# The last layer's bias added ahead of the transposes, and single stores in the last round

## The chip, the cores and the metric

The kernel runs on one core of one Trainium2 chip. Its time is the device time of one execution in microseconds (us), the median of several runs. TensorE (PE) multiplies into PSUM, ScalarE (ACT) and VectorE (DVE) do elementwise work, GpSimd (POOL) fills a few constants, and the queues of SyncE (SP) and ACT issue DMA transfers.

## The reference

A cross network of six layers on 4096 rows of 416 columns, in bfloat16:

```python
def reference(x0, ws, bs):          # x0 [4096, 416], ws [6, 416, 416], bs [6, 416]
    x = x0
    for l in range(ws.shape[0]):
        x = x0 * (x @ ws[l] + bs[l]) + x
    return x
```

With x = x0 * c, where c is a factor that starts at one, each layer is c <- c + (x @ ws[l] + bs[l]), and then x = x0 * c. So the kernel keeps the factor c beside x, and the output is x0 * (c + x @ ws[5] + bs[5]).

## The kernel before

**Layout.** Layers 0 to 4 work on transposed data: columns of the network on the 128 partitions, rows of the batch along the free dimension. 416 columns are three blocks of 128 (m = 0, 1, 2) and a remainder of 32. `XM0` holds x0 transposed, `CM` the factor c transposed, `XH` three half-batch buffers of x; `XR[0]`, `CR` and `XR` hold the same for the remainder, with the four groups of 512 rows stacked on the partitions. The batch has two halves, s = 0 and 1, of 2048 rows. The last layer (`LL` = 5) works on rows: 128 rows of the batch on the partitions, 416 columns free, so that its results can be stored as they are.

**A layer of the middle.** The six tiles (s, m) are named A = (0,0), B = (0,1), C = (0,2), D = (1,0), E = (1,1), F = (1,2). For each, TensorE fills two PSUM tiles of 128x1024 (`mm_full`, line 209; `mm_row`, line 215, for the remainder's share), taking them in pairs (`layer_products`). PSUM has room for four such tiles. ACT evicts each with its bias into a buffer of `t` (a pool of six), VectorE adds it to `CM` and multiplies by `XM0` into `XH`.

**The last such layer**, layer 4, is written out in `feeding_layer`, with VectorE's order given by hand: `pin` keeps a call in program order. `evict` is line 333, `add` line 341, `mul` line 345. It also prepares the last layer: a tile's factor `c` gets the last layer's bias (`last_bias`, line 349) and is then transposed by DMA from SP's queue into rows, `XLrows` (`xl_dmat`, line 232). The remainder goes through `CR`, `rem_out` and `scrR`, and ACT copies it to `XLrows` in `xl_rem` (line 312): `xl_rem(0)` just ahead of E's evictions, in `before_last`, and `xl_rem(1)` after F's. In the kernel before, `last_bias` covers all 2048 rows of a tile of s = 0, but for s = 1 only the first half of each group of 512, by a strided view of 4x256:

```python
            if s:
                c = c.rearrange("p (g r) -> p g r", g=NG)[:, :, 0:CW // 2]
```

**The last layer.** It has 32 blocks of 128 rows, in eight quads (s, i) of four blocks g; four rounds take two quads each. In each round TensorE forms eight products in eight PSUM banks: `mm_q_full` (line 464) for the three blocks of columns, `mm_q_rem` (line 477) for the remainder. For the two quads of s = 1 and i >= 2, that is, for the last round, `mm_q_rem` also adds the bias, as a product of a row of ones and the row `bLr` (line 481), since those rows of `CM` have no bias. ACT copies a product from PSUM to a buffer of `t` (line 507), VectorE adds `XLrows` (line 511) and multiplies by `X0rows` into an output tile (line 494, `close_product`, one block late), and the tile is stored (line 496). The first three rounds work by pairs of blocks, 128x832. The last round (`ENDS`) closes its eight blocks, u = 0 to 7, one at a time. For u >= 5 TensorE adds the factor itself, by products of `CM` and `CR` with an identity (lines 468 and 470), and line 511 falls away; u = 7 is multiplied by VectorE straight from PSUM. In the last round u = 0 to 5 are stored in pairs and u = 6 alone from SP's queue, u = 7 alone from ACT's.

The order of all of it is the program's order on each engine; waits between engines come from the tiles that they share. On SP the eight transposes of layer 4 stand ahead of all stores, in both kernels.

Of the kernel before, what the change touches and what calls it, by code (L numbers as in the profile page):

```python
# [9 lines left out]
ACT = mybir.ActivationFunctionType  # L10
ALU = mybir.AluOpType
BF16 = mybir.dt.bfloat16
# [4 lines left out]
def kernel(  # L17
# [7 lines left out]
    nc = tc.nc  # L25
    B, D = x0.shape
    L = ws.shape[0]
    P = 128
# [3 lines left out]
    NS = 2  # L32
    NG = 4
    CW = 512
    SW = NG * CW
# [11 lines left out]

    ident = const.tile([P, P], BF16)
    dz = const.tile([P, 2], FP32)
    ones = const.tile([P, P], BF16)  # L50
    WM = const.tile([P, L, NK, D], BF16)
    WR = const.tile([P, L, D], BF16)
    WD = const.tile([P, L, NG, R], BF16)
    bsb = const.tile([L, 4 * P], BF16)
    bLr = const.tile([P, D], BF16)
    bM = const.tile([P, NK, L], FP32)
    bR = const.tile([P, L], FP32)
    X0rows = big.tile([P, NBT, D], BF16)
# [21 lines left out]
    def pin(ins):  # L80
        tc.keep_in_program_order(ins)
# [18 lines left out]
    warm4 = nc.const_aps.tensor(1.0, [P, CW], FP32)  # L100
    nc.vector.memset(dz[:], 0.0)
    make_identity(nc, ident[:])
    nc.gpsimd.memset(ones[:], 1.0)
    nc.gpsimd.memset(WD[:], 0.0)

    load_x0t(0, 0)
# [21 lines left out]
        load_wr(nc.sync, g, 1, L)  # L128
    for l in range(2, L):
        load_wm(nc.sync, l)  # L130
    for q in range(18):
        b0, b1 = NBT * q // 18, NBT * (q + 1) // 18
        nc.sync.dma_start(X0rows[:, b0:b1, :], x0_v[:, b0:b1, :])
    for g in range(NG):
        nc.sync.dma_start(bLr[32 * g:32 * g + 1, :], bs[LL:LL + 1, :])

    def fill_wd(l0, l1):
        for g in range(NG):
# [92 lines left out]
    def xl_dmat(s, k):  # L231
        nc.sync.dma_start_transpose(out=XLrows[:, 16 * s:16 * s + 16, 128 * k:128 * k + 128],
                                    in_=CM[:, k, SW * s:SW * s + SW])
# [73 lines left out]
    def xl_rem(s):  # L307
        dst = XLrows[:, 16 * s:16 * s + 16, NK * P:D].rearrange("p (g i) r -> p i g r", g=NG)
        src = scrR[s][:].rearrange("p i (g r) -> p i g r", g=NG)
        n = 4 if s else 2  # L310
        for i in range(0, 4, n):
            pin(nc.scalar.copy(dst[:, i:i + n], src[:, i:i + n]))
# [13 lines left out]
    def feeding_layer(l, cur, curR, nxt, nxtR):  # L326
        tiles = [(s, m) for s in range(NS) for m in range(NK)]
        pts, ts = {}, {}

        def evict(t):  # L330
            for h in range(2):
                ts[t + (h,)] = tpool.tile([P, 2 * CW], BF16, name="t")
                nc.scalar.activation(ts[t + (h,)][:], pts[t][h][:].rearrange("p a b -> p (a b)"), ACT.Identity,  # L333
                                     bias=bM[:, t[1], l:l + 1], scale=1.0)

        def c_of(t, h):
            c0 = col0(t[0], 2 * h)
            return CM[:, t[1], c0:c0 + 2 * CW]

        def add(t, h):  # L340
            pin(nc.vector.tensor_tensor(out=c_of(t, h), in0=ts[t + (h,)][:], in1=c_of(t, h), op=ALU.add))  # L341

        def mul(t, h=0, n=2):
            c0, w = col0(t[0], 2 * h), n * CW
            pin(nc.vector.tensor_tensor(out=nxt[t[0]][:, t[1], 2 * CW * h:2 * CW * h + w], in0=CM[:, t[1], c0:c0 + w],  # L345
                                        in1=XM0[:, t[1], c0:c0 + w], op=ALU.mult))

        def last_bias(c, bias):
            pin(nc.vector.tensor_scalar(out=c, in0=c, scalar1=bias, scalar2=None, op0=ALU.add))

        def rows_out(t):
            s, m = t
            c = CM[:, m, SW * s:SW * s + SW]
            if s:
                c = c.rearrange("p (g r) -> p g r", g=NG)[:, :, 0:CW // 2]
            last_bias(c, bM[:, m, LL:L])
            xl_dmat(s, m)

        A, Bt, C, Dt, E, F = tiles
        layer_products(l, 0, tiles, pts, cur, curR, evict)  # L360
        evict(Bt)
        pr2 = psum.tile([P, 2, CW], FP32, tag="ps", name="pr2")
        for s in range(NS):
            mm_rem(l, s, pr2[:, s, :], cur, curR)
        tr = []
        for s in range(NS):
            tr.append(tpool.tile([P, 2 * CW], BF16, name="t"))
            for a in range(0, CW, CW // 2):
                nc.scalar.activation(tr[s][:, a:a + CW // 2], pr2[:, s, a:a + CW // 2], ACT.Identity, bias=bR[:, l:l + 1], scale=1.0)

        def rem(s, op):
            part = slice(CW * s, CW * s + CW)
            if op == ALU.add:
                pin(nc.vector.tensor_tensor(out=CR[:, part], in0=tr[s][:, 0:CW], in1=CR[:, part], op=op))
            else:
                pin(nc.vector.tensor_tensor(out=nxtR[:, part], in0=CR[:, part], in1=XR[0][:, part], op=op))

        def rem_out(s):
            last_bias(CR[:, CW * s:CW * s + (CW // 2 if s else CW)], bR[:, LL:L])
            nc.sync.dma_start_transpose(out=scrR[s][:], in_=CR[:, CW * s:CW * s + CW])  # L380

        add(A, 0)
        mul(A, 0)
        add(A, 1)
        add(Bt, 0)
        mul(A, 1)
        add(Bt, 1)
        rows_out(A)
        rem(0, ALU.add)
        mul(Bt, 0, 4)  # L390
        rem(0, ALU.mult)
        rem(1, ALU.add)
        rem_out(0)
        rows_out(Bt)
        rem(1, ALU.mult)

        layer_products(l, 2, tiles, pts, cur, curR, evict)
        evict(Dt)
        add(C, 0)
        add(C, 1)  # L400
        rem_out(1)
        mul(C, 0, 4)
        add(Dt, 0)
        add(Dt, 1)
        rows_out(C)
        mul(Dt, 0, 4)

        def before_last(t):
            xl_rem(0)
            evict(t)  # L410

        layer_products(l, 4, tiles, pts, cur, curR, before_last)
        evict(F)
        add(E, 0)
        rows_out(Dt)
        add(E, 1)
        mul(E, 0, 4)
        add(F, 0)
        add(F, 1)
        rows_out(E)  # L420
        mul(F, 0, 4)
        xl_rem(1)
        return lambda: rows_out(F)
# [22 lines left out]
    l = LL  # L446
# [25 lines left out]

    def mm_q_rem(q, py, done):
        s, i = quads[q]
        biased = s == NS - 1 and i >= 2
        for g in range(NG):
            nc.tensor.matmul(py[g][:, 0:D], lhsT=curR[32 * g:32 * g + 32, CW * s + 128 * i:CW * s + 128 * i + 128],  # L477
                             rhs=WR[32 * g:32 * g + 32, l, :], start=(g >= done), stop=(not biased and g < done),
                             tile_position=(32 * g, 0))
        for g in range(NG if biased else 0):  # L480
            nc.tensor.matmul(py[g][:, 0:D], lhsT=ones[32 * g:32 * g + 1, :],  # L481
                             rhs=bLr[32 * g:32 * g + 1, :], start=False, stop=(g < done), tile_position=(32 * g, 0))

    pending, outs = [], []

    def rows(q, g0, n):
        s, i = quads[q]
        b0 = 16 * s + 4 * g0 + i
        return slice(b0, b0 + 4 * (n - 1) + 1, 4)

    def close_product():
        while pending:
            src, q, g0, n, o, j, last, eng = pending.pop()
            pin(nc.vector.tensor_tensor(out=o[:, j:j + n, :], in0=src, in1=X0rows[:, rows(q, g0, n), :], op=ALU.mult))  # L494
            if last:
                eng.dma_start(out_v[:, rows(q, g0 - j, j + n), :], o[:, 0:j + n, :])

    def ew(q, g0, srcs, o, j, last, eng, added, direct):
# [20 lines left out]
    for q, at, done in rounds:  # L519
        tiles = [psum.tile([P, 2, CW], FP32, tag="ps", name=f"py{n}") for n in range(4)]  # L520
        bank = [tiles[n][:, a, :] for n, a in at]

        final = q + 2 == NQ

        def close(groups):
            u = groups[0][0]
            srcs = [tiles[at[g[0]][0]][:, at[g[0]][1]:at[g[0]][1] + len(g), 0:D] for g in groups]
            paired = final and u < 6
            j = u % 2 if paired else 0
            if not j:  # L530
                outs.append(opool.tile([P, 2, D], BF16, name="o"))
            ew(q + u // 4, u % 4, srcs, outs[-1], j, bool(j) or not paired, nc.scalar if final and u == 7 else nc.sync,
               final and u >= 5, final and u == 7)

        for u in range(done):
            if q == 0:
                mm_q_open(q, u, bank[u])
            else:
                mm_q_full(q, u, bank[u], False)
        mm_q_rem(q, bank[0:4], done)  # L540
        close([range(done)])
        if q == 0:
            last_rows_out()
        mm_q_rem(q + 1, bank[4:8], 0)
        for u in range(done, 8):
            mm_q_full(q + u // 4, u % 4, bank[u], True, final and u >= 5)
            if at is ENDS:
                close([[u]])
            elif u % 2:
                close([[u - 1, u]] if at is PAIRS else [[u - 1], [u]])  # L550
# [31 lines left out]
```

## Time and profile before

| | |
|---|---|
| median of 3 runs | 128.86 us (128.81 to 128.91) |
| the profiled execution | 129.12 us, its span 127.3 us |
| granted TensorE clock | 1.0 |
| busy: PE, DVE, ACT | 122.9, 102.4, 88.3 us |
| last byte of the last store written | 126.14 us |
| last landing | 126.51 us |

The span runs from the first to the last instruction that the profiler saw; the execution's time has some 1.8 us more around it. All times in what follows count from the span's start. Rows of groups give line, engine, operation, out<-in, partitions x elements and type, count, then busy us and mean ns of one, and the engine's idle time ahead of them with what ended it. Rows of a timeline give start, duration, engine, line, operation and count; equal instructions that follow each other are merged. On ACT and VectorE two neighbouring instructions overlap by a little under 0.1 us, so the cost of one in a full queue is the time from its start to the next start.

### The profile page before, as it was taken

To read this page: it belongs to the slowest core of one execution; us is meant where nothing else is said; L and a number is where in the kernel's file an instruction comes from. 1 tells how busy PE (TensorE), PEld (TensorE's weight loads), DVE (VectorE), ACT (ScalarE), POOL (GpSimd) and SP (SyncE) were. 2 spreads that over 40 slices of the span, in tenths; PEclk is the share of its full clock that TensorE was granted. 3 is DMA by queue.
4 is the path that set the end of the run, shared out by engine and by line. 5 is a ranking of instruction groups with operands and counts; after the bars stand their busy time and mean duration, and the time that the engine had idled before them with its cause. 6 is when DMAs were issued, how large, how long until landed. Compare 5 with 4: busy or idle time off the path is not lost.

```text
span 127.3 us, 3951 instructions
## 1 busy us (share of the span) xinstructions
PE 122.9 (97%) x1684; PEld 55.3 (43%) x1686; DVE 102.4 (80%) x192; ACT 88.3 (69%) x113; POOL 5.1 (4%) x18
## 2 busy tenths in 40 slices
PE   7999999999999999999999999999999999999980
PEld 3243343344534443444354445444534445445450
DVE  0033679674989898998898998898999999999991
ACT  0047866896869486869486859485859698679660
POOL 4004001400000000000000000000000000000000
PEclk9999999999999999999999999999999999999999
DMA  3999999999960000000000000000088999999865
GB/s 90 239 222 228 190 242 256 299 332 335 315 192 0 5 0 0 8 0 5 0 5 0 0 5 0 5 0 5 0 83 137 197 150 202 171 256 320 262 198 187
DMA packets 42230, 16.38 MB, mean 129 GB/s; under 512 B 31034, under 2 KB 42212, under 8 KB 42212
## 3 DMA queue, kind: packets, MB, share of 16 engines
q1 hardware_dynamic: 37432, 15.40, 53.3%
q10 hardware_dynamic: 4780, 0.72, 3.7%
q8 instruction: 13, 0.21, 0.7%
q14 instruction: 5, 0.04, 0.1%
HBM read 6.15 MB, written 3.41 MB: 75 GB/s over the span
## 4 chain that ended last, share of the span: by engine, by line
PE 90%; DMA 5%; SPq 1%; DVEq 1%; ACT 0%; issue 0%; DVE 0%
PE pt L209 50%; PE py L464 12%; PE ph L241 11%; DMA XM<-in_x_dram 5%; PE pt L215 5%; PE pr L225 5%; PE pr L221 2%; PE py L477 2%; PE ph L248 1%; SPq L78 1%; PE py L458 1%; DVEq L577 1%; ACT t L507 0%; PE py L481 0%; PE py L468 0%
## 5 line engine op out<-in xcount | busy, mean ns | idle before, releaser
L209 PE MATMUL pt<-XH,WM 128*32 128x512 bf16 x1152 | 65.2, 379 | 0.0
L187 ACT ACTIVATE t<-pt,bM 128x1024 bf16<-128x1024 f32 x36 | 37.2, 1115 | 13.1 <-PE pt L215 13.1
L209 PEld LDWEIGHTS <-WM 128*32 128x32 bf16 x1152 | 29.7, 97 | 33.8 <-issue 5.1
L188 DVE TENSOR_TENSOR CM<-t,CM 128x1024 bf16<-128x1024 bf16 x36 | 24.7, 687 | 4.3 <-ACT t L187 4.3
L189 DVE TENSOR_TENSOR XH<-CM,XM 128x1024 bf16<-128x1024 bf16 x36 | 24.9, 692 | 2.6
L507 ACT CAST t<-py 128x416 bf16<-128x416 f32 (+1 forms) x22 | 14.2, 649 | 4.2 <-PE py L464 2.0
L464 PE MATMUL py<-WM,XH 128*128 128x416 bf16 x90 | 17.0, 339 | 0.0
L241 PE MATMUL ph<-XM,WM 128*128 128x512 bf16 x70 | 16.3, 380 | 0.2
L333 ACT ACTIVATE t<-pt,bM 128x1024 bf16<-128x1024 f32 x12 | 12.4, 1115 | 4.1 <-PE pt L215 4.1
L181 ACT ACTIVATE CM<-ph,bM 128x1024 bf16<-128x1024 f32 x12 | 12.5, 1114 | 3.5 <-PE ph L248 3.5
L183 DVE TENSOR_TENSOR XH<-CM,XM 128x512 bf16<-128x512 bf16 x24 | 8.9, 430 | 4.5 <-ACT CM L181 4.5
L464 PEld LDWEIGHTS <-XH 128*128 128x128 bf16 x90 | 8.5, 98 | 7.5 <-issue 1.2
L241 PEld LDWEIGHTS <-WM 128*128 128x128 bf16 x72 | 6.7, 98 | 8.6 <-issue 1.3
L494 DVE TENSOR_TENSOR o<-t,X0rows 128x832 bf16<-128x832 bf16 (+1 forms) x19 | 9.4, 506 | 0.1
L511 DVE TENSOR_TENSOR t<-t,XLrows 128x832 bf16<-128x832 bf16 (+1 forms) x17 | 8.9, 523 | 0.0
L341 DVE TENSOR_TENSOR CM<-t,CM 128x1024 bf16<-128x1024 bf16 x12 | 8.0, 686 | 0.3 <-ACT t L333 0.3
L345 DVE TENSOR_TENSOR XH<-CM,XM 128x2048 bf16<-128x2048 bf16 (+1 forms) x7 | 7.5, 1068 | 0.2
L215 PE MATMUL pt<-XR,WR 32*128 32x512 bf16 x96 | 7.3, 379 | 0.0
L225 PE MATMUL pr<-XH,WM 128*32 128x512 bf16 x96 | 6.6, 379 | 0.0
L197 ACT ACTIVATE t<-pr,bR 128x256 bf16<-128x256 f32 (+1 forms) x16 | 5.3, 427 | 1.6 <-PE pr L225 1.6
L114 ACT ACT_TABLE_LOAD x1 | 1.3, 1283 | 6.1 <-DMA XM<-in_x_dram 6.1
L157 DVE CAST bM<-pb 128x18 f32<-128x18 bf16 x1 | 0.2, 177 | 5.5 <-PE pb L156 5.5
(61 smaller groups left out, 62.2 us busy)
## 6 DMA issues: line engine op xcount, KB each, us to landing
out_dram<-o SPq DMA_DIRECT2D x15, 208.0 KB, 2.9
X0rows<-in_x_dram SPq DMA_DIRECT2D x14, 208.0 KB, 4.4
WM<-in_ws_dram SPq DMA_DIRECT2D x5, 312.0 KB, 5.7
WR<-in_ws_dram SPq DMA_DIRECT2D x4, 130.0 KB, 3.9
X0rows<-in_x_dram SPq DMA_DIRECT2D x4, 104.0 KB, 5.4
WM<-in_ws_dram ACTq DMA_DIRECT2D x1, 312.0 KB, 3.3
XM<-in_x_dram SPq DMA_TRANSPOSE x8, 5.1
xrig<-in_x_dram ACTq DMA_DIRECT2D x4, 32.0 KB, 4.5
```

The lines of the kernel that those rows point to most:

```text
L181: nc.scalar.activation(c, src, ACT.Identity, bias=bias, scale=1.0)
L187: nc.scalar.activation(t[:], src, ACT.Identity, bias=bias, scale=1.0)
L188: nc.vector.tensor_tensor(out=c, in0=t[:], in1=c, op=ALU.add)
L189: nc.vector.tensor_tensor(out=x, in0=c, in1=XM0[:, m, c0:c0 + 2 * CW], op=ALU.mult)
L209: nc.tensor.matmul(pts[g // 2][32 * q:32 * q + 32, g % 2, :], lhsT=WM[:, l, k, 128 * m + 32 * q:128 * m + 32 * q + 32], rhs=cur[s][:, k, C ...
L215: nc.tensor.matmul(pts[g // 2][:, g % 2, :], lhsT=WR[32 * g:32 * g + 32, l, 128 * m:128 * m + 128], rhs=curR[32 * g:32 * g + 32, CW * s:CW ...
L225: nc.tensor.matmul(pr[32 * g:32 * g + 32, :], lhsT=WM[:, l, k, NK * P:D], rhs=cur[s][:, k, CW * g:CW * g + CW], start=False, stop=(k == NK ...
L241: nc.tensor.matmul(pt[:, gl, :], lhsT=WM[:, 0, k, 128 * m:128 * m + 128], rhs=cur[:, k, c0:c0 + CW], start=(k == 0 and not after_row), sto ...
L333: nc.scalar.activation(ts[t + (h,)][:], pts[t][h][:].rearrange("p a b -> p (a b)"), ACT.Identity, bias=bM[:, t[1], l:l + 1], scale=1.0)
L464: nc.tensor.matmul(py[:, 0:D], lhsT=q_x(q, g, k), rhs=WM[:, l, k, :], start=((not closes) and k == 0), stop=(closes and not adds and k == ...
L494: pin(nc.vector.tensor_tensor(out=o[:, j:j + n, :], in0=src, in1=X0rows[:, rows(q, g0, n), :], op=ALU.mult))
L507: nc.scalar.copy(t[:, n * D:n * D + w * D].rearrange("p (a d) -> p a d", a=w), src)
```

## The change

The last layer's bias is now added to the transposed factor for all rows, so the products with the row of ones go, and with them the tile `ones`, the row `bLr` and its four loads. To this end VectorE's additions on D, E and F and on the remainder of s = 1 cover all rows. For B and C the first 1024 rows are done by ACT, in place (`scalar_last_bias`), and VectorE does the second 1024. C's addition on ACT and its transpose stand in `before_last`, behind `xl_rem(0)` and ahead of E's evictions. B's product with x0 is made in two halves, the first ahead of its bias, and the additions and products of B stand in a new order. The remainder's evictions are pinned. In the last round only u = 4 and 5 are stored as a pair, u = 0 to 3 and 6 singly, and u = 7 in two halves of 64 partitions, one from SP's queue and one from ACT's. `X0rows` is loaded in 19 pieces instead of 18.

```diff
-    ones = const.tile([P, P], BF16)
-    bLr = const.tile([P, D], BF16)
-    nc.gpsimd.memset(ones[:], 1.0)
-    for q in range(18):
-        b0, b1 = NBT * q // 18, NBT * (q + 1) // 18
+    for q in range(19):
+        b0, b1 = NBT * q // 19, NBT * (q + 1) // 19
         nc.sync.dma_start(X0rows[:, b0:b1, :], x0_v[:, b0:b1, :])
-    for g in range(NG):
-        nc.sync.dma_start(bLr[32 * g:32 * g + 1, :], bs[LL:LL + 1, :])
...
-        def rows_out(t):
+        def scalar_last_bias(t):
+            pin(nc.scalar.activation(c_of(t, 0), c_of(t, 0), ACT.Identity, bias=bM[:, t[1], LL:L], scale=1.0))
+
+        def rows_out(t, skip=0):
             s, m = t
-            c = CM[:, m, SW * s:SW * s + SW]
-            if s:
-                c = c.rearrange("p (g r) -> p g r", g=NG)[:, :, 0:CW // 2]
-            last_bias(c, bM[:, m, LL:L])
+            last_bias(CM[:, m, SW * s + skip:SW * s + SW], bM[:, m, LL:L])
             xl_dmat(s, m)
...
         def rem_out(s):
-            last_bias(CR[:, CW * s:CW * s + (CW // 2 if s else CW)], bR[:, LL:L])
+            last_bias(CR[:, CW * s:CW * s + CW], bR[:, LL:L])
...
         mul(A, 1)
+        mul(Bt, 0)
+        rows_out(A)
+        scalar_last_bias(Bt)
         add(Bt, 1)
-        rows_out(A)
         rem(0, ALU.add)
-        mul(Bt, 0, 4)
+        mul(Bt, 1)
         rem(0, ALU.mult)
         rem(1, ALU.add)
         rem_out(0)
-        rows_out(Bt)
+        rows_out(Bt, 2 * CW)
         rem(1, ALU.mult)
...
-        rows_out(C)
+        last_bias(CM[:, C[1], SW * C[0] + 2 * CW:SW * C[0] + SW], bM[:, C[1], LL:L])
         mul(Dt, 0, 4)
 
         def before_last(t):
             xl_rem(0)
+            scalar_last_bias(C)
+            xl_dmat(*C)
             evict(t)
...
     def mm_q_rem(q, py, done):
         s, i = quads[q]
-        biased = s == NS - 1 and i >= 2
         for g in range(NG):
...
-        for g in range(NG if biased else 0):
-            nc.tensor.matmul(py[g][:, 0:D], lhsT=ones[32 * g:32 * g + 1, :],
-                             rhs=bLr[32 * g:32 * g + 1, :], start=False, stop=(g < done), tile_position=(32 * g, 0))
...
-            if last:
+            if eng is None:
+                for e, part in ((nc.sync, slice(0, P // 2)), (nc.scalar, slice(P // 2, P))):
+                    e.dma_start(out_v[part, rows(q, g0, 1), :], o[part, 0:1, :])
+            elif last:
                 eng.dma_start(out_v[:, rows(q, g0 - j, j + n), :], o[:, 0:j + n, :])
...
-            paired = final and u < 6
+            paired = final and u in (4, 5)
```

More of the change, by code (lines that the diff above doesn't have):

```diff
@@ L368, in feeding_layer @@
             for a in range(0, CW, CW // 2):
-                nc.scalar.activation(tr[s][:, a:a + CW // 2], pr2[:, s, a:a + CW // 2], ACT.Identity, bias=bR[:, l:l + 1], scale=1.0)
+                pin(nc.scalar.activation(tr[s][:, a:a + CW // 2], pr2[:, s, a:a + CW // 2], ACT.Identity,
+                                         bias=bR[:, l:l + 1], scale=1.0))
         def rem(s, op):
@@ L474, in mm_q_rem @@
         s, i = quads[q]
-        biased = s == NS - 1 and i >= 2
         for g in range(NG):
             nc.tensor.matmul(py[g][:, 0:D], lhsT=curR[32 * g:32 * g + 32, CW * s + 128 * i:CW * s + 128 * i + 128],
-                             rhs=WR[32 * g:32 * g + 32, l, :], start=(g >= done), stop=(not biased and g < done),
+                             rhs=WR[32 * g:32 * g + 32, l, :], start=(g >= done), stop=(g < done),
                              tile_position=(32 * g, 0))
-        for g in range(NG if biased else 0):
-            nc.tensor.matmul(py[g][:, 0:D], lhsT=ones[32 * g:32 * g + 1, :],
-                             rhs=bLr[32 * g:32 * g + 1, :], start=False, stop=(g < done), tile_position=(32 * g, 0))
     pending, outs = [], []
@@ L531, in close @@
                 outs.append(opool.tile([P, 2, D], BF16, name="o"))
-            ew(q + u // 4, u % 4, srcs, outs[-1], j, bool(j) or not paired, nc.scalar if final and u == 7 else nc.sync,
+            ew(q + u // 4, u % 4, srcs, outs[-1], j, bool(j) or not paired, None if final and u == 7 else nc.sync,
                final and u >= 5, final and u == 7)
```

## The prediction

> **What bounds the kernel now.** I read the page's busy shares and slices first, then the chain that ended last, then the groups by form for prices, then the timelines of DVE and ACT over the last 35 us, and last the windows with the DMA share.
>
> Busy shares and the DVE slices of the page:
>
> ```profile
> PE 122.9 (97%) x1684; PEld 55.3 (43%) x1686; DVE 102.4 (80%) x192; ACT 88.3 (69%) x113; POOL 5.1 (4%) x18
> DVE  0033679674989898998898998898999999999991
> ```
>
> TensorE is full, but VectorE's digits turn to an unbroken 9 for 11 slices before the last one (3.18 us each, so from about 89 us on). The chain of waits, its end:
>
> ```profile
> 118.93 0.18 PE py L481 x4
> 119.11 0.18 PE py L477 x4
> 119.28 0.18 PE py L481 x4
> ...
> 123.15 0.52 ACT t L507
> 123.66 0.02 issue
> 123.68 0.04 DVE o L494
> ```
>
> The chain stays on TensorE to 123.1, so the two 0.18 pieces of L481, the bias products that go, are on it. After that it runs through ACT's last copy and two VectorE products. Prices, from the groups by form:
>
> ```profile
> L333 ACT ACTIVATE t<-pt,bM 128x1024 bf16<-128x1024 f32 x12 | 12.4, 1115 | 4.1 <-PE pt L215 4.1
> L349 DVE TENSOR_SCALAR CM<-CM,bM 128x2048 bf16<-128x2048 bf16 x3 | 2.2, 747 | 0.0
> L349 DVE TENSOR_SCALAR CM<-CM,bM 128x1024 bf16<-128x1024 bf16 x3 | 1.4, 482 | 0.0
> L312 ACT COPY XLrows<-scrR 128x512 bf16<-128x512 bf16 x1 | 0.6, 632 | 0.0
> ```
>
> Half a bias addition is 0.27 us cheaper (747 against 482 ns). VectorE around tiles E and F, ACT before E, and VectorE's end, from the timelines:
>
> ```profile
> 101.99 0.69 DVE L341 TENSOR_TENSOR CM<-t,CM 128x1024 bf16<-128x1024 bf16 x1
> 102.60 0.48 DVE L349 TENSOR_SCALAR CM<-CM,bM 128x1024 bf16<-128x1024 bf16 x1
> 102.99 0.68 DVE L341 TENSOR_TENSOR CM<-t,CM 128x1024 bf16<-128x1024 bf16 x1
> ```
>
> ```profile
> 98.98 0.71 ACT L312 COPY XLrows<-scrR 128x256 bf16<-128x256 bf16 x2
> 100.73 3.12 ACT L333 ACTIVATE t<-pt,bM 128x1024 bf16<-128x1024 f32 x3 [1.04 <-PE pt L215]
> ```
>
> ```profile
> 122.67 1.38 DVE L494 TENSOR_TENSOR o<-t,X0rows 128x416 bf16<-128x416 bf16 x4
> 123.97 0.58 DVE L494 TENSOR_TENSOR o<-py,X0rows 128x416 bf16<-128x416 f32 x1
> ```
>
> VectorE goes from one row to the next without a gap; ACT has 1.04 us free just before E's evictions. The last transfers, from the windows (the last two columns are DMA share and GB/s):
>
> ```profile
> 121.00:123.90 2.90, 2.83 (x25) 1.75 (x23) 2.83 (x11) 2.19 (x5) 0.00 (x0) 1.00 0.61 196
> 124.50:125.40 0.90, 0.00 (x0) 0.00 (x0) 0.06 (x1) 0.00 (x0) 0.00 (x0) 1.00 0.96 314
> ```
>
> After 123.9 the stores, not the engines, fill the time: a share of 0.96, where it was 0.61.
>
> **TensorE, removed.** Eight products with the row of ones, four at a time: two steps of 0.18 on the chain, 0.36 us. The first set falls ahead of round 3's first closing, so ACT's copy of u=0 comes 0.18 earlier; all later copies can come 0.36 earlier. ACT's last copy would end at 123.29 instead of 123.65. Nothing of this is worth anything unless VectorE takes those tiles earlier.
>
> **VectorE, added.** Start to start, a 2048-wide bias addition takes 0.66 (92.31 to 92.97), a 1024-wide one 0.40 (102.60 to 102.99). Tile B loses 0.27 and C 0.27 to ACT. D, E and F gain 0.27 each. `rem_out(1)` goes from 256 to 512 columns (281 to 348 ns), +0.07. `mul(Bt)` in two halves costs 2 x 0.60 instead of 1.14, +0.07. In all +0.40, but order matters more than the sum:
> - What B saves, 0.20 net, is lost at the addition of C's second half: it starts at 97.05 and its operand's eviction ends at 97.02, so it cannot move.
> - From there, rem_out +0.07 and C's -0.27 would bring VectorE to `add(E, 0)` at 101.80 instead of 101.99. E's first eviction starts at 100.73 on TensorE's word and takes 1.115, so it ends at 101.85. With the 0.03 that VectorE takes after such an end, 101.88. The saving there is 0.11, not 0.20.
> - After it nothing waits on ACT again for a long while, and D, E, F add 0.80. By the second addition of the last layer (108.56 before) VectorE is 0.69 late.
>
> In the last rounds VectorE waited five times for ACT in the trace before: start to start less the usual step of the same instruction, at 117.63 (0.03), 118.69 (0.04), 119.77 (0.08), 120.67 (0.10: 0.60 instead of 0.50) and 123.68 (0.15). That is 0.40. A late VectorE swallows all five, and has nothing more to swallow. 0.69 - 0.40 = 0.29: its last product ends at 124.85 instead of 124.56. TensorE's 0.36 turns into copies that lie waiting. The six buffers of `t` hold these: each copy's slot was freed at least 0.9 us before by this schedule.
>
> **ACT, added.** Two activations of 128x1024 from SBUF, of which the trace has none. From below, L312's copies step 0.31 for 256 columns and 0.51 for 512, which goes on to 0.90 for 1024. From above, L333, which reads PSUM: 1.115 alone, 1.01 start to start. I take 1.0, since L333 has the same operation and width. B's goes behind the remainder's evictions (free at 93.44) and ahead of C's (94.90): 1.45 us of room, hidden. C's stands between `xl_rem(0)` and E's evictions. `xl_rem(0)` waits for a transpose that landed at 98.96 in the trace, and `rem_out(0)` ends 0.07 later in the new order, so it starts at 99.05 and frees ACT at 99.67; with 1.0, E's eviction could start at 100.67, 0.06 ahead of TensorE. So it costs nothing by this, and up to 0.05 by the upper price; every tenth beyond goes straight to `add(E, 0)` and the end. The Trainium skill (ScalarE: Activation LUTs, What ACT_TABLE_LOAD costs) gives about 280 ns + 0.833 ns a column with a pointer bias, 93 ns of it overlapped, so an estimate of 1.04 here and E's eviction at 100.71; L333's 1.115 is near its 1.13, and no row here shows an SBUF source. By it the sum stays as it is.
>
> **SP and the transposes.** XL(C) now also waits for ACT's half, done about 100.8; SP is busy with the previous transpose to 100.96 anyway (101.03 with the 0.07). XL(E) waited for VectorE (106.64), and goes 0.42 later, XL(F) behind it too. F's packets ended at 113.68; they are wanted by VectorE at 115.59, so 1.9 us covers 0.4. The first stores move 0.4 later as well, and the queue catches up by about 119. The loads of X0rows are 19 instead of 18 and four tiny loads go: all by 36 us, wanted at 109, so nothing.
>
> **Stores.** From the trace's packet records, before: the transfer for u=2,3 (256 rows of 832 B) begins at 123.96, 0.89 after its issue at 123.07; from there 768 rows run almost without a hole to 126.14, a pair taking 0.70. The last landing is at 126.51, the span ends at 127.30. With singles and VectorE's new times: u=0 to 3 are issued at 121.8, 122.4, 123.0 and 123.5 and have run out by 124.8. The pair u=4,5 is issued at 124.09 and begins at 124.97, with 512 rows left from there: 1.40 us at the rate above, 126.37, and 0.08 more if the two queues get in each other's way as u=6 and u=7 did. So the last byte is 0.23 to 0.31 later. SP needs 0.37 plus 0.06 a store and gets one each 0.57, so it holds, until u=7's half: it waits for u=6's issue and starts at about 125.03, ACT's half at 124.88. Splitting u=7 gives nothing in this, because engines at 0.96 have no room.
>
> The Trainium skill (DMA: Bandwidth & Descriptors, Rules for kernel authors) says that two transfers of disjoint partition halves serialize, both spreading over the same 16 engines. It speaks against this edit. The trace's 314 GB/s with both queues active fits it; the case where halves do help is the third rival.
>
> **Sum.** VectorE's end +0.29, last byte +0.23 to +0.31, C's activation 0 to +0.05: +0.29. The profiled execution took 129.12 (span 127.3 and 1.8 around it), so its like would be 129.41; on the median of 128.86, **129.15**. 0.2% (0.26 us) is about what a measurement of this kernel can tell from no change; the forecast is just over it.
>
> **Rivals.**
> 1. *TensorE's 0.36 reaches the end: 128.5.* This needs VectorE to be less than 0.04 late at 117.6, where I have 0.69. For it: the chain names TensorE. Against it: no gap over 0.15 in VectorE's rows from 88.5 on. It decides at 0.40 of lateness, where the five waits are used up. Chance 0.07.
> 2. *ACT's addition to C holds E's evictions.* A late transpose or an activation of 1.25 makes them start 0.1 to 0.4 late, and VectorE and F's eviction with them, for which TensorE already waited 0.1 at 104.91. 129.25 to 129.55; chance 0.18.
> 3. *The relieved store queue gives VectorE's delay back.* With singles out of the way u=7 needs no more than its 0.89 and its own 0.35: issued at 124.88, done at 126.12, level with before. That needs u=4 to 6 to run faster than 0.35 per 128 rows, or the halves to overtake them. 128.85 to 129.05, no change; chance 0.30. If VectorE also recovers 0.3, it becomes faster, 128.55; chance 0.04.
> 4. *SP falls behind with singles,* as with the 1.21 us issue at 116.71: u=7's half 0.5 late, 129.65. Chance 0.04.
>
> The forecast has 0.37, its own range 129.05 to 129.25, which straddles the 0.2%: a quarter of it, about 0.09, counts as same. Faster 0.07 + 0.04 = 0.11. Same 0.30 + 0.09 = 0.39. Slower 0.28 + 0.18 + 0.04 = 0.50. The range from 128.70 to 129.50 leaves out the faster cases and the ends of 2 and 4.
>
> **What would show it.** Right: `add(E, 0)` near 101.9, the second addition of the last layer near 109.2, VectorE without a gap from there to its last product at 124.85, ACT's last copy ending about 0.7 before VectorE takes it, and the last landing near 126.8. Wrong: an idle time over 0.1 on VectorE behind 117, or E's eviction released by ACT's own queue instead of by TensorE, or a last landing that does not follow VectorE's end.

## The result, and the profile after

The changed kernel takes 130.37 us, median of 4 runs (130.12 to 130.48), against 128.84 for the kernel before beside it: a ratio of 1.0114, 95% interval 1.0100 to 1.0128. It is slower by 1.5 us where 0.3 was forecast. The profiled execution took 130.12 with a span of 128.3, 1.0 longer than the one before.

The page's busy line and VectorE's slices after, and one group that waits as it did not before:

```profile
PE 122.7 (96%) x1676; PEld 55.1 (43%) x1678; DVE 102.8 (80%) x193; ACT 90.4 (70%) x115; POOL 4.5 (4%) x17
DVE  0023479874989898988898989898999999999990
...
L236 PE MATMUL ph<-XM,WM 128*128 128x512 bf16 x70 | 16.6, 382 | 0.5 <-ACT CM L176 0.4
```

The end looks as forecast: TensorE is 0.2 us less busy, VectorE at 9 for the last slices but one. The group is the surprise. It is layer 0, at the very start, which the prediction did not touch: TensorE now waits there for ACT's eviction. The same group, and the head of the chain of waits (start, length, what), before:

```profile
L241 PE MATMUL ph<-XM,WM 128*128 128x512 bf16 x70 | 16.3, 380 | 0.2
```

```profile
2.18 6.66 DMA XM<-in_x_dram
8.84 0.04 issue
8.88 2.10 PE ph L241 x9
```

After, the chain comes to TensorE's products through ACT:

```profile
6.78 4.53 DMA XM<-in_x_dram
11.31 0.02 issue
11.33 0.02 ACTq L89
11.35 0.04 issue
11.39 0.67 ACTq L89
12.06 0.05 issue
12.11 1.12 ACT CM L176
13.23 0.04 issue
13.27 0.38 PE ph L236
```

L89 is ACT's issue of the load of `xrem`. It waits until 11.33 for a transpose of x0, with whose data it has nothing to do. Behind it on ACT's queue stands layer 0's first eviction, and behind that TensorE, which needs the PSUM. ACT's timeline before, and after:

```profile
10.59 0.62 ACTq L91 DMA_DIRECT2D xrem<-in_x_dram  x1
11.35 4.13 ACT L181 ACTIVATE CM<-ph,bM 128x1024 bf16<-128x1024 f32 x4 [0.35 <-PE ph L248]
```

```profile
11.39 0.67 ACTq L89 DMA_DIRECT2D xrem<-in_x_dram  x1
12.11 3.12 ACT L176 ACTIVATE CM<-ph,bM 128x1024 bf16<-128x1024 f32 x3 [1.28 <-PE ph L243]
```

ACT's first eviction starts 0.76 later. The profile names a product of TensorE as the releaser, since that is what came last by its account; but ACT had the issue of L89 ahead of it, and that one was late.

The issue records in the traces name the semaphores, and so show what L89 waits for. The transfers of this program share eight completion semaphores ("lanes"), handed out in turn in the order in which the scheduler places the transfers, and a transfer on a lane is issued only when the one before it there has landed. Before, the load of `xrem` came second behind layer 1's WM and had the lane of WR's small first load, landed at 9.9. In the changed program it comes third, and has the lane of the fourth transpose of x0, landed at 11.31. The loads behind it in that order do not enter. Which edit moved it is left to the runs below.

VectorE and ACT around tile E, after; they answer to the rows shown of before:

```profile
102.31 0.69 DVE L336 TENSOR_TENSOR CM<-t,CM 128x1024 bf16<-128x1024 bf16 x1
102.92 0.75 DVE L344 TENSOR_SCALAR CM<-CM,bM 128x2048 bf16<-128x2048 bf16 x1
103.58 0.69 DVE L336 TENSOR_TENSOR CM<-t,CM 128x1024 bf16<-128x1024 bf16 x1
```

```profile
99.34 0.72 ACT L307 COPY XLrows<-scrR 128x256 bf16<-128x256 bf16 x2
99.96 1.15 ACT L347 ACTIVATE CM<-CM,bM 128x1024 bf16<-128x1024 bf16 x1
101.17 2.12 ACT L328 ACTIVATE t<-pt,bM 128x1024 bf16<-128x1024 f32 x2
```

All of this stands 0.37 later than before because of the start. Counted from the first eviction of A in layer 4 (87.33 before, 87.71 after), `add(E, 0)` comes 0.05 earlier, and VectorE's last product ends 37.52 later instead of 37.23. The end on VectorE, and SP's last two entries (the first merges the pair and u = 6, the second is SP's half of u = 7):

```profile
123.52 1.21 DVE L490 TENSOR_TENSOR o<-t,X0rows 128x416 bf16<-128x416 bf16 x4
124.66 0.57 DVE L490 TENSOR_TENSOR o<-py,X0rows 128x416 bf16<-128x416 f32 x1
```

```profile
124.51 0.90 SPq L495 DMA_DIRECT2D out_dram<-o  x2
125.50 0.56 SPq L493 DMA_DIRECT2D out_dram<-o  x1
```

VectorE ends at 125.23; SP issues its half 0.27 later, behind the issue of u = 6; it lands at 127.50, 2.27 behind VectorE's end instead of 1.95. So the two profiled spans differ by 0.37 at the start, 0.29 on VectorE and 0.32 at the stores. All runs below are given against the kernel before on the same chip (median 128.94 to 128.97).

### The profile page after: what moved, and what is told of

It is laid out like the page before. It is cut to its first block, busy times and chain, and to the rows that moved or that the text cites. A ratio compares the mean times of both kernels' runs of the same rounds, so it can differ in the third digit from the quotient of the medians.

```text
span 128.3 us, 3946 instructions
## 1 busy us (share of the span) xinstructions
PE 122.7 (96%) x1676; PEld 55.1 (43%) x1678; DVE 102.8 (80%) x193; ACT 90.4 (70%) x115; POOL 4.5 (4%) x17
## 4 chain that ended last, share of the span: by engine, by line
PE 68%; DVE 16%; SPq 5%; DMA 4%; issue 3%; ACT 1%; ACTq 1%; DVEq 0%
PE pt L204 47%; PE ph L236 8%; DVE t L510 5%; PE pr L220 5%; PE pt L210 5%; DVE o L490 5%; SPq L76 5%; DMA XM<-in_x_dram 4%; DVE XH L340 3%; DVE CM L336 2%; PE pr L216 2%; DVE CM L344 1%; PE ph L243 1%; ACT CM L176 1%; ACTq L89 1%
## 5 line engine op out<-in xcount | busy, mean ns | idle before, releaser
L340 DVE TENSOR_TENSOR XH<-CM,XM 128x1024 bf16<-128x1024 bf16 (+1 forms) x8 | 7.5, 953 | 0.2
```

## Experiments

**The start.** First the deleted memset is put back, with everything else as changed.

```diff
+    ones = const.tile([P, P], BF16)
     make_identity(nc, ident[:])
+    nc.gpsimd.memset(ones[:], 1.0)
```

> The changed kernel with the unused tile of ones and its GpSimd memset (0.2 us) kept; in the build the load of xrem then waits for no earlier transfer on its completion lane, as in the kernel before. Lane theory: ACT issues that load near 10.6 us instead of 11.4, TensorE's idle 0.35 us at 13.3 goes, and the time falls by 0.37, from 130.37 to 130.0. Rival, the late start is only the spread between executions: 130.3 to 130.4, and the load's wait is seen or not seen at random.

Measured: 129.67, ratio 1.0057 (1.0040 to 1.0075). The load is issued at 10.59 and TensorE's wait for ACT is gone. It brings back 0.57% or 0.73 us, twice what the one trace showed. Next the same thing the other way round, on the kernel before:

```diff
-    nc.gpsimd.memset(ones[:], 1.0)
     nc.gpsimd.memset(WD[:], 0.0)
+    nc.gpsimd.memset(ones[:], 1.0)
```

> The kernel before with one line moved: the memset of ones behind that of WD. In the build the load of xrem then gets another completion lane, whose earlier transfer is a transpose of x0. Nothing of the arithmetic, VectorE's work or the stores differs. Lane theory: TensorE stalls about 0.35 us at 13 us and all later work moves by it, 128.84 to 129.2. Rival, GpSimd's order cannot matter since GpSimd is idle from 2 to 5 us: 128.84.

Measured: 130.28, ratio 1.0102 (1.0086 to 1.0117). One line that computes the same, on an engine with 4% load, costs 1.3 us. At the start its trace has the wait (issue at 11.39), and TensorE's stall of 0.33. That leaves a good part over, and it lies at the end (see the last run). To separate the lane from the memset, two changed kernels without the memset. One puts a transfer more ahead of the load:

```diff
-    for g in range(NG):
+    load_wr(nc.sync, 0, 1, 2)
+    load_wr(nc.sync, 0, 2, L)
+    for g in range(1, NG):
         load_wr(nc.sync, g, 1, L)
```

> The changed kernel with one load of WR (32 partitions, five layers) made as two, layer 1 and the rest: the same bytes, one transfer more ahead of xrem's load in the order of the program, which moves xrem's completion lane one on, to that of the fifth transpose of x0. That one landed at 13.72 in the changed kernel's trace. Lane theory: ACT issues xrem's load at about 13.8 instead of 11.4, its first eviction moves from 12.1 to 14.5, TensorE stalls some 2.4 us longer: 132.5 to 133. Rival, GpSimd's memset of ones mattered by itself and lanes do not: 130.4.

Measured: 132.75, ratio 1.0314 (1.0273 to 1.0356). ACT's timeline of this kernel:

```profile
14.05 0.65 ACTq L89 DMA_DIRECT2D xrem<-in_x_dram  x1
14.74 1.11 ACT L178 ACTIVATE CM<-ph,bM 128x1024 bf16<-128x1024 f32 x1 [3.54 <-DMA XM<-in_x_dram]
```

The issue moves on to 14.05, and with ACT idle for 3.54 the profile now names the transpose itself. TensorE stalls 2.64. The other one moves the loads of WR ahead of a load of WM, so that the lane is free:

```diff
-    load_wm(nc.sync, 1)
     for g in range(NG):
         load_wr(nc.sync, g, 1, L)
+    load_wm(nc.sync, 1)
```

> The changed kernel, still without the tile of ones, with the four loads of WR ahead of layer 1's WM on SP's queue: in the build xrem's load then waits for no earlier transfer. Stores, biases and VectorE's work are those of the changed kernel. Lane theory: as with the memset kept, 129.6 to 129.8. Rival, the memset itself: 130.4. Layer 1's WM lands about 2 us later, at 23, and is wanted at 26.7, so it costs nothing.

Measured: 129.79, ratio 1.0070 (1.0057 to 1.0084), issue at 10.41. So the lane is the cause, and GpSimd's memset matters only through the order that the scheduler makes. How large is the term? The first eviction of A in layer 4 starts at 87.01 to 87.33 in nine traces with a free lane (mean 87.15), and at 87.70 to 88.09 in four on the fourth transpose's lane (mean 87.85): 0.7 us, as the times say. In this spread the profiled execution before stood at the late end and the one after at the early end, which hid half of the term.

**The stores and the end.** The changed kernel with the stores of before:

```diff
-            paired = final and u in (4, 5)
+            paired = final and u < 6
-            ..., None if final and u == 7 else nc.sync,
+            ..., nc.scalar if final and u == 7 else nc.sync,
```

> The changed kernel with the last round's stores as in the kernel before: pairs for u = 0 to 5, u = 6 alone from SP, u = 7 alone from ACT. Theory that SP's queue falls behind with single stores: the last landing follows VectorE's end by 1.95 us instead of 2.27, so 130.37 falls to 130.05. Rival of the forecast, that the singles relieve the transfers: pairs push the last byte back and the time stays or rises, 130.4 to 130.6.

Measured: 130.32, ratio 1.0103 (1.0087 to 1.0119), within the interval of the changed kernel. Both expectations missed. The same with the memset kept:

> Both at once: the memset of ones kept and the stores as before; what is left of the change is the bias on all rows, ACT's two additions and the removed products. Theory of three separate delays (start 0.37, VectorE 0.30, stores 0.32, read from the two traces): only VectorE's is left, 128.84 + 0.30 = 129.1. Rival, a fourth cause that the profiled execution of the changed kernel shows less of (its three other runs took 0.3 more): 129.4 to 129.7.

Measured: 129.57, ratio 1.0046 (1.0033 to 1.0058): inside the rival's range, so more than VectorE's term was left. Its trace shows what, and why the stores seemed to matter little. Its last landing is 2.12 behind VectorE's end, better than 2.27; but the span ends 1.02 behind that landing and not 0.83. At the end SP waits for the lanes in a fixed order, 0.065 each, and the last store sat on a lane with three others behind it (with four loads fewer and one more the lanes had moved by three). Loading X0rows in 22 pieces puts it back on the last lane:

```diff
-    for q in range(19):
-        b0, b1 = NBT * q // 19, NBT * (q + 1) // 19
+    for q in range(22):
+        b0, b1 = NBT * q // 22, NBT * (q + 1) // 22
```

> The bias change alone (ones memset kept, stores as before), with the loads of X0rows in 22 pieces, so that the number of transfers and with it the completion lane of the last store is that of the kernel before. Theory that the closing waits go over the lanes in a fixed order, 0.065 us each, and that three of them came behind the last landing when that store had an earlier lane: the span ends 0.84 us behind the last landing instead of 1.02, 129.57 falls to 129.4, and VectorE's 0.25 to 0.30 is what is left. Rival, the piece count does nothing: 129.55.

Measured: 129.33, ratio 1.0030 (1.0020 to 1.0041), and 0.83 again from landing to end. This is the change of the bias alone, free of lanes and stores: +0.39 us (0.26 to 0.53). On it the two edits of the stores, one at a time, each with the last store on the last lane (`X0rows` in 20 and 21 pieces). First u = 0 to 3 singly, u = 7 still in one store:

> As the kernel with the bias change alone, with the same lane for the last store, but u = 0 to 3 stored singly; u = 7 stays one store from ACT's queue. Theory that only the half of u = 7 behind u = 6 on SP is late: the last landing follows VectorE's end by 1.95 to 2.1, 129.4, the same as with pairs. Rival, singles cost by themselves through SP's issue time: u = 6 lands after u = 7, 129.5 to 129.6. Rival of the forecast, singles relieve the transfers: 129.2.

Measured: 129.38, ratio 1.0036 (1.0024 to 1.0048). Single stores cost nothing that can be told, and relieve nothing. Then u = 0 to 5 in pairs, and u = 7 in two halves:

> As the kernel with the bias change alone, but u = 7 stored in two halves, from SP and ACT; u = 0 to 5 in pairs. Theory that SP's half waits for SP's issue of u = 6: it starts 0.2 after ACT's and lands last, 2.25 behind VectorE's end, 129.6. Rival, two halves move in half the time: 129.2 to 129.3.

Measured: 129.71, ratio 1.0057 (1.0046 to 1.0068): the two halves cost 0.27% or 0.35 us. In the trace ACT's half is issued at 124.61, SP's at 124.82 behind u = 6, and they land at 126.57 and 126.86. A half takes as long from issue to landing, 1.97 and 2.04, as the whole does (1.92 before, 2.12 in the bias-only kernel). Of the 0.35 this trace shows 0.14, the landing 2.29 behind VectorE's end instead of 2.15: its execution was the fastest of six, and where the rest lies is not shown.

**VectorE.** On the bias-only kernel the 0.80 that D, E and F had gained is taken off VectorE again. The first half of the rows of D, E and F then goes without the last layer's bias, so this kernel is for its time alone:

```diff
             s, m = t
+            skip = max(skip, s * SW // 2)
             last_bias(CM[:, m, SW * s + skip:SW * s + SW], bM[:, m, LL:L])
```

> The same kernel, but VectorE adds the last layer's bias only to the second half of the rows of D, E and F (1024 columns instead of 2048); the other half of the rows of s = 1 goes without that bias. VectorE theory: 0.8 us less on VectorE, TensorE's 0.36 now reaches the end: the last product ends at 124.2 instead of 124.8, 128.8 to 128.9. Rival, VectorE is not what holds the end: the time stays at 129.4.

Measured: 128.83, ratio 0.9995 (0.9984 to 1.0005), 0.35% below the bias-only kernel. VectorE's last rows, first of the bias-only kernel, then of this:

```profile
122.87 1.22 DVE L492 TENSOR_TENSOR o<-t,X0rows 128x416 bf16<-128x416 bf16 x4
124.01 0.58 DVE L492 TENSOR_TENSOR o<-py,X0rows 128x416 bf16<-128x416 f32 x1
```

```profile
122.34 1.22 DVE L493 TENSOR_TENSOR o<-t,X0rows 128x416 bf16<-128x416 bf16 x4
123.48 0.58 DVE L493 TENSOR_TENSOR o<-py,X0rows 128x416 bf16<-128x416 f32 x1
```

From A's first eviction to the end of the last product it is 37.52 in the one and 36.93 in the other: 0.59 for the 0.80 taken off, as VectorE then meets ACT's copies again. So it is VectorE that held the end.

**A version to beat both.** From that reading, work moved off VectorE in two more places, with nothing left out: the first half of E's bias goes to ACT, and the factor of u = 4 in the last round to TensorE:

```diff
         add(E, 1)
         mul(E, 0, 4)
+        xl_rem(1)
+        scalar_last_bias(E)
         add(F, 0)
         add(F, 1)
-        rows_out(E)
+        rows_out(E, 2 * CW)
         mul(F, 0, 4)
-        xl_rem(1)
...
-            ... True, final and u >= 5)
+            ... True, final and u >= 4)
```

> A version that is to beat both: the bias change alone with lanes and stores as before, with the first half of E's bias on ACT behind xl_rem(1) (0.27 less on VectorE) and with u = 4 of the last round given its factor by TensorE too (VectorE 0.29 less, TensorE 0.23 more). VectorE theory: it is then 0.13 late instead of 0.69, TensorE's end is 0.13 earlier than before, and the last product ends 0.15 earlier: 128.75. Rival, ACT's copies, now 1.0 later at 105, hold TensorE in round 1: 129.2.

Measured: 129.21, ratio 1.0018 (1.0009 to 1.0027). It does not beat the kernel before. The rival's time came true, but not its reason: TensorE was not held, and VectorE did what was expected (37.12 from A's eviction to its end, 0.11 less than before). But the last landing came 2.26 behind it. The last nine rows of data left one by one, 125.66 to 125.98, as if a single DMA engine had been behind.

**The late landing.** The same pattern was in the kernel with the moved memset, so that kernel was run again.

> The kernel before with the memset of ones behind that of WD, looked at a second time. Its first trace had 0.36 at the start and another 0.72 behind VectorE's last product, where one instruction fetch of 8 KB ran from 124.5 to 125.1 among the last stores. Theory that this fetch recurs in this program and slows one of the 16 DMA engines: a last landing 2.6 us behind VectorE's end again. Rival, chance: 1.95 to 2.1 behind it, and a time near 129.5.

Measured: 130.59 in one run; the landing is 2.66 behind VectorE's end, 2.67 the first time. In both an 8 KB instruction fetch runs for 0.6 us while the last stores are in the engines (124.51 to 125.13, 124.90 to 125.54), SP's issue of u = 6, which falls into it, takes 0.81 and 0.84 us instead of 0.43, and the last rows follow one by one. In the kernel before the last such fetch began at 126.07, when all but the last rows were out. From its issue to its landing the last store took 2.63 us in both, against 1.92 before.

That the late landing recurs in this program is shown, in two traces of two. The other traces with u = 7 in one store fit the fetch as well: where the last fetch begins 0.9 to 1.7 us ahead of the last store's issue, the last store takes 1.99 to 2.12 us; at 0.64 ahead (the version to beat both) 2.22; at 0.44 and 0.45 ahead the 2.63. But no run took the fetch away, so that it causes the lag is not shown, and what moved it (the added wait is one more instruction on ACT's sequencer) is open.

## Why the prediction was wrong

Lane 0.57%, bias 0.30%, halves and singles 0.27% make 1.14%, the measured ratio. As differences from one run to the next (changed, memset kept, bias alone, before) they must add up. What checks them stands apart from that: the lane by the start of layer 4 (0.7 us), and the halves and the singles by themselves on the bias-only kernel (0.27%, and 0.06%, which is not told from nothing). The forecast had a fifth of the whole. Both terms that it set at nothing mattered: with the lane free the time is still 0.73 us longer than before, where 0.3 was forecast; the bias alone is 0.39.

- **The step that failed** is the one that set the removed start-up work at nothing. It went through the loads ("all by 36 us, wanted at 109, so nothing") and not through the memset at all. Both were judged by data and engine time, and there the judgement holds. Removing the memset moved the order of the program, the order gave out other lanes, and the lane made ACT's queue wait. The wait stood in the changed program, one semaphore more on the load of `xrem`, and its price in the trace of before: a transpose that lands at 11.50, with ACT's first eviction, due at 11.35, behind it. None of the rivals was of this kind; the largest term had no chance in the range.
- **VectorE: right in mechanism; its size came out right partly by luck.** VectorE was late without a gap, swallowed its waits for ACT, and held the end; taking work off it let TensorE's gain through. The forecast times of `add(E, 0)` (101.88), the second addition of the last layer (109.25) and the end of ACT's last copy (123.29) are met to 0.01 in the trace with the memset kept, but there layer 4 starts 0.06 earlier than before. Counted from A's first eviction, `add(E, 0)` gained 0.05 instead of 0.11, the second addition came 0.75 later instead of 0.69, and ACT's last copy 0.30 earlier instead of 0.36. The waits that VectorE swallowed come to 0.45 instead of 0.40, so that the end is 0.30 later, 0.29 by the forecast: two errors of 0.05 to 0.06 cancel.
- **ACT: the price was low, the conclusion held.** In place in SBUF the activation takes 1.14 to 1.17, not 1.0. The Trainium skill's estimate for it, 1.13 alone by ScalarE: Activation LUTs (What ACT_TABLE_LOAD costs), was closer than the row I chose. Still it is TensorE that releases E's eviction, and the second rival is out: in all eleven traces with the new bias that eviction starts 13.46 behind A's first one (13.40 before), whether ACT's addition ended 0.07 ahead of it or 0.10 behind its start. The 0.06 is a wait for TensorE that stands on ACT's queue as an instruction of its own, 0.06 ahead of the eviction; before, the eviction carried that wait itself. This is the 0.06 that `add(E, 0)` did not gain.
- **Stores: the term was mis-sized.** "SP needs 0.37 plus 0.06 a store and gets one each 0.57, so it holds": the step from issue to issue was 0.45 to 0.56 and SP was late for u = 6 by 0.25 already. The fourth rival foresaw a late half, but by the singles, and these are not the reason: with pairs, in the bias-only kernel, SP is late for u = 6 by 0.21, against 0.05 before, because VectorE, no longer waiting, ends the products of u = 5 and 6 only 0.29 apart. And the last byte was reckoned from the load of the engines, at 1.40 us for 512 rows, so that a late half did not matter. The runs show about 2 us from the last issue to its landing instead, for 64 rows or 128. So what counts is when the last store is issued, and the half from SP is issued 0.2 later. It measured 0.35, not the 0 of the forecast.
- The rule that two partition halves serialize (the Trainium skill, DMA: Bandwidth & Descriptors, Rules for kernel authors) fits the packet records of the run with halves alone: ACT's half leaves from 125.83 to 126.18, SP's from 126.10 to 126.46, though SP's was also issued later. The halves were not neutral but a loss, 1.0057 against 1.0030. The third rival, singles that relieve the queue, is out by 1.0036 against 1.0030, and the first by VectorE's 0.75.
- Not foreseen, and small: the lane of the last store, 0.19 in two of the experiments and 0.1 in the one with the lane one further, none in the changed kernel itself, whose last store again had the last lane.

Left open are the landings 2.02 to 2.15 behind VectorE's end in the kernels with the new bias and u = 7 in one store, against 1.95 before: about 0.1 of the bias-only kernel's 0.39.

## What to carry to other kernels

Before an edit's removed or added transfers and constants are set at nothing, compare the waits of every issuing queue in the two builds, above all where compute stands behind the issue: a transfer may wait for another one with which it shares only a completion semaphore. Cost a VectorE that runs without gaps by its sequence, from the last place where it must wait, and not by the sum of the added work. For the last store, count from its issue: here one store from an idle queue was better than two halves of which one stood behind another issue.

## What the runs showed of the hardware that was not expected

- A transfer issued from ACT's queue held ACT's compute for as long as its completion semaphore was in use: 0.76 us with the fourth transpose's (first eviction at 12.11 against 11.35), 3.4 us with the fifth's (14.74). The Trainium skill (DMA: Bandwidth & Descriptors, Why a DMA increments its semaphore by 16 and not by 1) warns that two transfers in flight on one semaphore can mix their counts, and asks for one semaphore for each in flight; the waits here keep to that.
- A store of 64 rows of 832 bytes took as long to land as one of 128: 1.97 to 2.04 us against 1.92 to 2.12, late landings aside. Part of that is its issue: ACT's issue of u = 7 took 0.54 to 0.56 us as a half and 0.38 whole.
- The closing waits cost 0.065 us for each lane that was checked behind the last one to land: 0.19 us for three.
- An activation of 128x1024 in place in SBUF took 1.14 to 1.17 us, the same from PSUM 1.11.
- One line moved on an engine with 4% load changed the time by 1.0%, and it did so again: 130.28 and 130.59 against 128.97 and 128.96.
